# Attention with a gated GLU, forward and backward: one padded weight load per head, and two more natural layouts by crossbar transposes

## The chip, the cores and the metric

The kernel runs on one core of one Trainium2 chip. The metric is the device time of one execution in microseconds (us), as the median of three runs.

## The reference

The forward part normalises x (2048 rows of 576), runs attention of 32 heads over a given cache of 2048 keys and values of width 128, and gates the result:

```python
xn = layernorm(x)
q  = (xn @ wq) per head; p = softmax(q @ k_cache^T * Dh**-0.5); s = (p @ v_cache) @ wo
b  = (sigmoid(xn @ w_gate) * (xn @ w_up)) @ w_down          # F = 4608
out = x + s * silu(b)
```

What is computed is this output and, for a given `grad_out`, the gradients of all of x, k_cache, v_cache, wq, wo, w_gate, w_up and w_down. All inputs and outputs are bf16.

## The kernel before

The program goes through six stages, one after the other.

1. **Gate and up products** (span time 0 to 331 us). The rows stand in 16 row tiles of 128. A loop over (column group, row tile) multiplies a row tile of xn^T by 512 columns of w_gate and w_up at a time and stores the results `h_row` and `a_row` (four buffers each) to DRAM from GpSimd. Beside it runs a "guard": SP loads pieces of k_cache and wq into `x_all`, VectorE and ScalarE square them, and a flag says at the end whether the softmax may leave out its maximum. The order of each engine's instructions here is that of the program.
2. **Down product** (331 to 485): the gate's value and its derivative for each row tile, and dS^T (`dsT`), the gradient before wo. The loads of head 0 start here.
3. **Attention, forward and backward** (485 to 3532). It is made of slots, 32 for each of 32 heads. Slot qt of the first 16 (`main1`) multiplies Q's row tile qt with all keys in two halves and ScalarE exponentiates them into a slab Pq of 128 x 2048; SP turns the slab by a crossbar transpose (`transpose_slab`, line 630). Six slots later (`SKEW`) `tail1` multiplies the turned slab with V. The second 16 slots (`main2`) do the same with dO and V: dP, dS in place of P, a second turn, and `tail2` with K, six slots later. The gradients of V and K are sums over the slabs (`Partial`, line 744) whose stationary operands are dO and Q in natural layout (row on the partition), scaled per row by `scale_don` and `scale_qn`.
4. **Output projection** (3532 to 3677): 16 row tiles; each turns its row of the attention output from DRAM by `load_oT` on SP, into one of three places `oTs`.
5. **GLU backward** (3677 to 4542).
6. **Gradients of wq, wo and x** (4542 to 4945), in eight groups of four heads. SP turns wq's columns (`wqT`) and the rows of dQ (`dqbT`); each group takes eight steps of 32 pairs of matmuls. In the last two groups (`early` and `final`) eight row tiles each of x's gradient are finished between the steps, from step `wait_n` on (`ends_rows`, `finish`); VectorE does most of a finished row. `early` uses also the next group's `wqT2` and `dqbT2`.

Attention takes its order from `plan(h)`: `put(slot, cost, fn)` hangs small units of work on slots, so that the next head is prepared while the last one runs. Before the change these units are, for each head: K and V in four loads each; wo's rows (two loads into `wo_h`) and wq's columns (two loads), all from GpSimd; a crossbar transpose of `wo_h` into `woT` (line 208); four `prep_qt` (Q^T = wq^T xn^T) and four `prep_dot` (dO^T = wo dS^T); crossbar transposes of K and V (`turn_nat`); and two steps that take the natural layouts from the transposed ones on TensorE:

```python
def prep_don(hs, sc):   # four times a head: 4 transposes of 128 x 128, one copy by VectorE
def prep_qn(hs):        # once a head: 16 transposes, two copies by VectorE
```

Both go through `pe_transpose_blocks`, line 145. The attention output and dQ are stored from GpSimd after every fourth row tile (`G4`, `store_nat`, line 677).

Of the kernel before, what the change touches and what calls it, by code (L numbers as in the profile page):

```python
# [9 lines left out]
bf = mybir.dt.bfloat16  # L10
# [3 lines left out]
P = 128  # L14
# [52 lines left out]
def kernel(  # L67
# [41 lines left out]
    dq2_d = dram.tile([S, HD], bf, name="dq2_d")  # L109
    kvT_d = dram.tile([H, 2, P, S], bf, name="kvT_d")  # L110
# [40 lines left out]
    def new_head(h):  # L151
        hs = HeadState()
        hs.h = h
        hs.wq, hs.woT = wqs[h % 2], woTs[h % 2]
        hs.Kn = Kns[h % 2]
        hs.Vn, hs.VT, hs.KT, hs.QT, hs.dOT, hs.dOn, hs.Qn = Vn, VT, KT, QT, dOT, dOn, Qn
        return hs

    def load_wq(hs):
        hcols = slice(hs.h * P, (hs.h + 1) * P)  # L160
        nf = DT - 1 if KPAD else DT
        if nf:
            nc.gpsimd.dma_start(hs.wq[:, :nf, :], A_wq[:nf * P, hcols].rearrange("(i p) c -> p i c", p=P))
        if KPAD:
            nc.gpsimd.dma_start(hs.wq[LO:, nf, :], A_wq[nf * P:, hcols])

    def load_wo(hs):
        nf = (DT - 1) * P if KPAD else D
        rows = slice(hs.h * P, (hs.h + 1) * P)
        if nf:  # L170
            nc.gpsimd.dma_start(wo_h[:, :nf], A_wo[rows, :nf])
        if KPAD:
            nc.gpsimd.dma_start(wo_h[:, nf + LO:], A_wo[rows, nf:])
# [11 lines left out]
    def prep_loads(h):  # L185
        hs = new_head(h)
        load_wq(hs)
        load_wo(hs)
        load_k(hs)
        load_v(hs)  # L190
        return hs
# [8 lines left out]

    def prep_wot(hs):
        pt = acc_tile(bf)
        for i in range(DT):
            nc.tensor.transpose(pt[:, i, :], wo_h[:, i * P:(i + 1) * P], ident[:])
        alt.copy(hs.woT[:], pt[:, :DT, :], eng="s")

    def turn_wot(hs):
        nc.sync.dma_start_transpose(hs.woT[:], wo_h[:])
# [25 lines left out]
    with tc.tile_pool(name="pa", bufs=1) as pa:  # L234
# [75 lines left out]
        with tc.tile_pool(name="a1w", bufs=1) as wp:  # L310
# [37 lines left out]
            with tc.tile_pool(name="a0", bufs=3) as sb0, tc.tile_pool(name="a0ps", bufs=2, space=PSUM) as ps0, \  # L348
# [55 lines left out]

                todo = {"norm": list(range(min(LA + 2, L1), L1)), "turn": list(range(LA, L1)), "bn": list(range(L1, NT))}
# [26 lines left out]
                for n_row, (gi, st) in enumerate(rows_order):  # L432
# [41 lines left out]
                    if gi > 1 and st % 2 and wd_left:  # L474
                        load_wd()
                assert begin is not None
# [4 lines left out]
                while wd_left:  # L481
                    load_wd()
                guard_end()
# [12 lines left out]
        wqs = [pdT.tile([P, DT, P], bf, name=f"wq_h{b}") for b in range(2)]  # L496
        woTs = [pdT.tile([P, DT, P], bf, name=f"woT_h{b}") for b in range(2)]
        for t_ in wqs:
            zlow(t_)
        wo_h = pdT.tile([P, DT * P], bf, name="wo_h")  # L500
        if KPAD:
            nc.gpsimd.memset(wo_h[:, (DT - 1) * P:(DT - 1) * P + LO], 0.0)
# [3 lines left out]
        with tc.tile_pool(name="a2h", bufs=3) as hp, \  # L506
# [49 lines left out]
            prep_wot(heads_pre[0])  # L556
# [31 lines left out]
    G4 = min(4, NT)  # L588
# [4 lines left out]
    def attention(fast):  # L593
        with ExitStack() as es:
# [19 lines left out]
            def turn_nat(dst, src):  # L614
                nc.sync.dma_start_transpose(dst[:].rearrange("p (t q) -> p t q", q=P), src[:].rearrange("p t d -> p (t d)"))

# [170 lines left out]
            def plan(h):  # L787
# [3 lines left out]
                if h:  # L791
                    put(pl, 0, lambda: heads.__setitem__(h, start_head(h)))
                    for c in range(4):
                        put(pl + q(c), 0, lambda c=c: load_k(hd(), c, 4))
                        put(pl + q(skew + 3 + c), 0, lambda c=c: load_v(hd(), c, 4))
                    put(pl + q(4), 0, lambda: load_wo(hd()))
                    put(pl + q(5), 0, lambda: load_wq(hd()))
                    put(pl + q(NTH + 3), 0, lambda: turn_nat(hd().KT, hd().Kn))
                    put(pl + q(skew + 4), 0, lambda: turn_wot(hd()))
                    for sc in range(NSC):  # L800
                        put(pl + q(skew + 4 + 2 * sc), DT * CH, lambda sc=sc: prep_qt(hd(), sc))
# [3 lines left out]
                for sc in range(NSC):  # L805
                    put(b1 + q(sc), DT * CH, lambda sc=sc: prep_dot(hd(), sc))
                    put(b1 + q(sc + 1), nb * P, lambda sc=sc: prep_don(hd(), sc))
                for qt in range(NT):
                    put(b1 + max(qt + 1, q(2 + qt // nb)), 0, lambda qt=qt: scale_don(hd(), qt))
                put(b1 + q(NTH + 3), 0, lambda: turn_nat(hd().VT, hd().Vn))  # L810
                put(b1 + q(NTH + 2), NT * P, lambda: prep_qn(hd()))
# [70 lines left out]
    with late("pc") as pc, late("pcf") as pcf, \  # L882
# [22 lines left out]
        with late("c1l3", 4) as ldp3, late("c1s", 2) as sb, \  # L905
# [34 lines left out]
            for st in range(1, R0):  # L940
                nc.gpsimd.tensor_copy(oTs[st][0:1, 0, 0:1], loads[0][st % 3][0:1, 0:1])
                load_oT(oTs[st], st)
# [217 lines left out]
        with late("c2w") as wp, late("c2b") as blk, late("c2s", 2) as sb, late("c2ps", 4, space=PSUM) as ps:  # L1160
# [45 lines left out]
            for hg in range(NHG):  # L1206
# [6 lines left out]
                for a in range(NTE if final else 0, NT, NQ):  # L1213
                    turn_rows(dqbT, dqb, a, min(a + NQ, NT), HG)
# [4 lines left out]
                wait_n = min(5 if early else 2, nsteps - 2)  # L1219
# [11 lines left out]
                for hl in range(HG):  # L1231
# [4 lines left out]
                    if early and hl == min(1, HG - 1):  # L1236
                        nc.sync.dma_start_transpose(wqT2[:], A_wq[:, (hg + 1) * HC:(hg + 2) * HC])
                        turn_rows(dqbT2, onqs[(hg + 1) % 2][1], 0, NTE, HG)
# [51 lines left out]
```

## Time and profile before

| | |
|---|---|
| median of three runs | 4960.12 us (4959.86 to 4975.73) |
| the profiled execution | 4946.58 us, its span 4944.8 us |
| TensorE busy | 4874.4 us, 99% |
| VectorE, ScalarE, GpSimd busy | 57%, 50%, 17% |
| granted TensorE clock, mean | 0.997 |
| DMA packets under 512 B | 2951889 of 3048180 |
| crossbar transposes of P and dS | 512 and 512, median 5.0 and 5.1 us to landing |

The span runs from the first instruction to the last; the time of an execution includes what lies around it. TensorE's matmuls overlap one another, so that its busy time does not tell how close it is to its pace. The distance between the starts of successive matmuls tells that.

### The profile page before, as it was taken

To read this page: it belongs to the slowest core of one execution; us is meant where nothing else is said; L and a number is where in the kernel's file an instruction comes from. 1 tells how busy PE (TensorE), PEld (TensorE's weight loads), DVE (VectorE), ACT (ScalarE), POOL (GpSimd) and SP (SyncE) were. 2 spreads that over 40 slices of the span, in tenths; PEclk is the share of its full clock that TensorE was granted. 3 is DMA by queue.
4 is the path that set the end of the run, shared out by engine and by line. 5 is a ranking of instruction groups with operands and counts; after the bars stand their busy time and mean duration, and the time that the engine had idled before them with its cause. 6 is when DMAs were issued, how large, how long until landed. Compare 5 with 4: busy or idle time off the path is not lost. (4 is left out here: it accounts for less than half of the span.)

```text
span 4944.8 us, 101626 instructions
## 1 busy us (share of the span) xinstructions
PE 4874.4 (99%) x41029; PEld 2893.5 (59%) x41029; DVE 2801.6 (57%) x6554; ACT 2474.9 (50%) x4228; POOL 842.3 (17%) x1330
## 2 busy tenths in 40 slices
PE   9999999999999999999999999999899999999998
PEld 4445566666666666666666666666455555555554
DVE  4544666666566666666656656666434555553224
ACT  4432666766676676676676667667212111111111
POOL 3322111111111111111111111111221111111111
PEclk9999999999999999999999999999999999999999
DMA  7887999999999999999999999999999999997765
GB/s 260 274 202 175 219 222 227 227 228 226 228 231 226 228 228 232 225 228 229 224 229 231 230 222 231 225 226 231 216 221 238 224 226 223 234 235 185 205 175 131
DMA packets 3048180, 1097.68 MB, mean 222 GB/s; under 512 B 2951889, under 2 KB 2956114, under 8 KB 3047698
## 3 DMA queue, kind: packets, MB, share of 16 engines
q1 hardware_dynamic: 2948930, 771.66, 83.4%
q0 software_dynamic: 98160, 318.85, 20.3%
q8 instruction: 322, 5.28, 0.4%
q14 instruction: 160, 1.31, 0.1%
q10 hardware_dynamic: 608, 0.59, 0.0%
HBM read 175.31 MB, written 177.93 MB: 71 GB/s over the span
## 5 line engine op out<-in xcount | busy, mean ns | idle before, releaser
L654 ACT ACTIVATE Pq<-sp 128x1024 bf16<-128x1024 f32 x1024 | 1048.1, 1024 | 267.2 <-PE sp L636 258.1
L709 DVE SCALAR_TENSOR_TENSOR Pq<-dp,negdelta,Pq 128x1024 bf16<-128x1024 f32 x512 | 654.9, 1279 | 42.9 <-PE dp L706 42.9
L712 ACT ACTIVATE t<-dp,negdelta 128x1024 bf16<-128x1024 f32 x512 | 567.6, 1115 | 214.3 <-PE dp L706 199.8
L636 PE MATMUL sp<-KQ 128*128 128x512 bf16 x2048 | 609.7, 379 | 2.2 <-ACT Pq L654 2.1
L706 PE MATMUL dp<-VT,dOT 128*128 128x512 bf16 x2048 | 609.2, 379 | 2.3
L683 PEld LDWEIGHTS <-dST 128*128 128x128 bf16 x8192 | 508.1, 98 | 150.7 <-DMA dST<-Pq 9.9
L683 PEld LDWEIGHTS <-PT 128*128 128x128 bf16 x8192 | 500.2, 98 | 134.7 <-DMA PT<-Pq 14.0
L683 PE MATMUL acc<-Kn,dST 128*128 128x128 bf16 x8192 | 557.1, 219 | 5.7 <-DMA dST<-Pq 5.7
L683 PE MATMUL acc<-Vn,PT 128*128 128x128 bf16 x8192 | 542.4, 219 | 9.9 <-DMA PT<-Pq 9.6
L713 DVE TENSOR_TENSOR Pq<-t,Pq 128x1024 bf16<-128x1024 bf16 x512 | 354.5, 692 | 316.7 <-ACT t L712 306.2
L744 PE MATMUL acc<-Pq,dOn 128*128 128x512 bf16 x2048 | 531.7, 379 | 0.0
L744 PE MATMUL acc<-Pq,Qn 128*128 128x512 bf16 x2048 | 525.7, 379 | 0.0
L724 ACT ACTIVATE dq_n<-acc,rsc 128x128 bf16<-128x128 f32 x512 | 187.7, 367 | 331.5 <-PE acc L683 310.1
L1153 DVE TENSOR_TENSOR dxn<-acc,dxn 128x576 f32<-128x576 f32 x272 | 206.1, 758 | 248.2 <-PE acc L1053 248.2
L744 PEld LDWEIGHTS <-Qn 128*128 128x128 bf16 x2048 | 200.3, 98 | 240.4 <-issue 0.8
L744 PEld LDWEIGHTS <-dOn 128*128 128x128 bf16 x2048 | 199.0, 98 | 234.2 <-DVE dOn L669 0.3
L1115 ACT ACTIVATE ndh<-dh 128x512 bf16<-128x512 f32 x144 | 86.0, 597 | 452.5 <-DVE du_blk L1113 448.7
L641 DVE TENSOR_REDUCE rs_all<-rsp 128x1 f32<-128x2 f32 x512 | 78.3, 153 | 307.3 <-ACT Pq L654 295.8
L636 PEld LDWEIGHTS <-KQ 128*128 128x128 bf16 x2048 | 179.2, 98 | 124.1 <-issue 3.9
L706 PEld LDWEIGHTS <-dOT 128*128 128x128 bf16 x2048 | 178.7, 98 | 124.2 <-issue 11.7
L677 POOL DMA_DIRECT2D on_d<-o_n x128 | 97.3, 760 | 784.8 <-DVE junk L695 460.3
L677 POOL DMA_DIRECT2D dq_d<-dq_n x128 | 98.1, 766 | 716.9 <-ACT dq_n L724 677.1
(209 smaller groups left out, 6820.8 us busy)
## 6 DMA issues: line engine op xcount, KB each, us to landing
out_dram<-kvn POOLq DMA_DIRECT2D x64, 512.0 KB, 4.6
ah<-a_d POOLq DMA_DIRECT2D x18, 1024.0 KB, 9.5
ah<-h_d POOLq DMA_DIRECT2D x18, 1024.0 KB, 12.1
h_d<-h_row POOLq DMA_DIRECT2D x64, 256.0 KB, 3.4
a_d<-a_row POOLq DMA_DIRECT2D x64, 256.0 KB, 3.8
x_all<-in_A_k_cache_dram SPq DMA_DIRECT2D x64, 256.0 KB, 3.7
on_d<-o_n POOLq DMA_DIRECT2D x128, 128.0 KB, 4.7
kvT_d<-KQ POOLq DMA_DIRECT2D x32, 512.0 KB, 5.5
```

Of the source, the lines that this page charges most:

```text
L636: nc.tensor.matmul(sp[:, c * CH:(c + 1) * CH], lhsT=hs.QT[:, qt * P:(qt + 1) * P], rhs=hs.KT[:, hf * HW_ + c * CH: hf * HW_ + (c + 1) * CH ...
L654: nc.scalar.activation(Pq[:, hsl], sp[:], AF.Exp, scale=SCALE, accum_out=hs.rsp[:, hf:hf + 1])
L677: nc.gpsimd.dma_start(dst_d[q0 * P:(qt + 1) * P, hs.h * P:(hs.h + 1) * P].rearrange("(t p) d -> p t d", p=P), buf[:])
L683: nc.tensor.matmul(hs.acc[:, 0, :], lhsT=T[:, kt, :], rhs=rhs[:, kt, :], start=(kt == 0), stop=(kt == NT - 1))
L706: nc.tensor.matmul(dp[:, c * CH:(c + 1) * CH], lhsT=hs.dOT[:, qt * P:(qt + 1) * P], rhs=hs.VT[:, hf * HW_ + c * CH: hf * HW_ + (c + 1) * C ...
L709: nc.vector.scalar_tensor_tensor(Pq[:, hsl], dp[:], hs.negdelta[:, qt:qt + 1], Pq[:, hsl], op0=ALU.add, op1=ALU.mult)
L712: nc.scalar.activation(t[:], dp[:], AF.Identity, bias=hs.negdelta[:, qt:qt + 1], scale=1.0)
L713: nc.vector.tensor_tensor(Pq[:, hsl], t[:], Pq[:, hsl], op=ALU.mult)
L724: nc.scalar.activation(hs.dq_n[:, qt % G4, :], hs.acc[:, 0, :], AF.Copy, scale=hs.rsc[:, qt:qt + 1])
L744: nc.tensor.matmul(self.acc, lhsT=self.nat[:, qt, :], rhs=self.slabs[qt][:, cs], start=(qt == self.lo), stop=(qt == self.hi - 1))
L1115: nc.scalar.mul(ndh[:], dh[:], -1.0)
L1153: nc.vector.tensor_tensor(dxn[:, st, :], acc[:, :D], dxn[:, st, :], op=ALU.add)
```

## The change

- A DRAM copy `w2_d` holds, for each head, wq's columns and the transposed rows of wo, padded to 5 x 128. It is made in stage 1: `w2_load` brings two heads' wq by GpSimd and turns wo's rows by SP out of DRAM, and one call later `w2_store` clears the padding and stores both. The calls come after every second row from row 18 on. In attention one load per head (`load_w2`) takes the place of four loads and the turn of `wo_h`; head 0's transposes of wo on TensorE go too.
- K and V of the next head are loaded in two halves, not four quarters.
- The attention output and dQ are stored after every eighth row tile.
- `prep_don` and `prep_qn` go. `turn_T` makes dO (in two halves, in slots 2 and 4) and Q (in slot 9) in natural layout by crossbar transposes on SP. `scale_don` starts two slots after its half.
- In the output projection, GpSimd's one-element copy that held back `load_oT` of row tile 1 goes; that for row tile 2 stays.
- In the last stage `early` turns `wqT2` and `dqbT2` ahead of the second half of its own rows, and the final rows start at step 3 (before: 5) and 1 (before: 2).

```diff
-    def load_wq(hs):
...
-    def load_wo(hs):
...
+    def load_w2(hs):
+        nc.gpsimd.dma_start(hs.w2[:], w2_d[hs.h])
...
-    def turn_wot(hs):
-        nc.sync.dma_start_transpose(hs.woT[:], wo_h[:])
...
+                def w2_load():
+                    if w2_left:
+                        hh = w2_left.pop(0)
+                        n = len(hh)
+                        t_ = sb0.tile([P, 2, 2, DT, P], bf, name="w2", bufs=2)
...
+                        for k in range(n):
+                            hc = slice(hh[k] * P, (hh[k] + 1) * P)
+                            if nf2:
+                                nc.gpsimd.dma_start(t_[:, k, 0, :nf2, :], A_wq[:nf2 * P, hc].rearrange("(i p) c -> p i c", p=P))
+                                nc.sync.dma_start_transpose(t_[:, k, 1, :nf2, :], A_wo[hc, :nf2 * P])
+                            if KPAD:
+                                nc.gpsimd.dma_start(t_[LO:, k, 0, nf2, :], A_wq[nf2 * P:, hc])
+                                nc.sync.dma_start_transpose(t_[:, k, 1, nf2, :], A_wo[hc, D - P:])
+                        w2_wait.append((t_, hh))
+
+                def w2_store():
...
+                            nc.gpsimd.memset(t_[:LO, :n, :, nf2, :], 0.0)
+                        nc.gpsimd.dma_start(w2_d[hh[0]:hh[-1] + 1].rearrange("h p k i c -> p h (k i c)"),
+                                            t_[:, :n].rearrange("p h k i c -> p h (k i c)"))
...
+                    if n_row > NT and n_row % 2 == 0:
+                        w2_store()
+                        w2_load()
...
-            prep_wot(heads_pre[0])
...
-    G4 = min(4, NT)
+    G4 = ldiv(NT, 8)
...
+            def turn_T(dst, src, lo, hi):
+                nc.sync.dma_start_transpose(dst[:, lo:hi, :], src[:, lo * P:hi * P])
...
-                    for c in range(4):
-                        put(pl + q(c), 0, lambda c=c: load_k(hd(), c, 4))
-                        put(pl + q(skew + 3 + c), 0, lambda c=c: load_v(hd(), c, 4))
-                    put(pl + q(4), 0, lambda: load_wo(hd()))
-                    put(pl + q(5), 0, lambda: load_wq(hd()))
+                    for c in range(2):
+                        put(pl + q(2 * c), 0, lambda c=c: load_k(hd(), c, 2))
+                        put(pl + q(skew + 3 + 2 * c), 0, lambda c=c: load_v(hd(), c, 2))
+                    put(pl + q(4), 0, lambda: load_w2(hd()))
...
-                    put(pl + q(skew + 4), 0, lambda: turn_wot(hd()))
...
-                    put(b1 + q(sc + 1), nb * P, lambda sc=sc: prep_don(hd(), sc))
+                NDON = 2 if NSC % 2 == 0 else 1
+                for c in range(NDON):
+                    put(b1 + q((c + 1) * NSC // NDON), 0, lambda c=c: turn_T(hd().dOn, hd().dOT, c * NT // NDON, (c + 1) * NT // NDON))
                 for qt in range(NT):
-                    put(b1 + max(qt + 1, q(2 + qt // nb)), 0, lambda qt=qt: scale_don(hd(), qt))
+                    put(b1 + max(qt + 1, q((qt * NDON // NT + 1) * NSC // NDON + 2)), 0, lambda qt=qt: scale_don(hd(), qt))
...
-                put(b1 + q(NTH + 2), NT * P, lambda: prep_qn(hd()))
+                put(b1 + q(NTH + 1), 0, lambda: turn_T(hd().Qn, hd().QT, 0, NT))
...
-                nc.gpsimd.tensor_copy(oTs[st][0:1, 0, 0:1], loads[0][st % 3][0:1, 0:1])
+                if st > 1:
+                    nc.gpsimd.tensor_copy(oTs[st][0:1, 0, 0:1], loads[0][st % 3][0:1, 0:1])
                 load_oT(oTs[st], st)
...
-                for a in range(NTE if final else 0, NT, NQ):
-                    turn_rows(dqbT, dqb, a, min(a + NQ, NT), HG)
+                def turn_dq(a, b):
+                    for a_ in range(a, b, NQ):
+                        turn_rows(dqbT, dqb, a_, min(a_ + NQ, b), HG)
+                turn_dq(NTE if final else 0, NTE if early else NT)
+                if early:
+                    nc.sync.dma_start_transpose(wqT2[:], A_wq[:, (hg + 1) * HC:(hg + 2) * HC])
+                    turn_rows(dqbT2, onqs[(hg + 1) % 2][1], 0, NTE, HG)
...
-                wait_n = min(5 if early else 2, nsteps - 2)
+                wait_n = min(3 if early else 1, nsteps - 2)
...
                     if early and hl == min(1, HG - 1):
-                        nc.sync.dma_start_transpose(wqT2[:], A_wq[:, (hg + 1) * HC:(hg + 2) * HC])
-                        turn_rows(dqbT2, onqs[(hg + 1) % 2][1], 0, NTE, HG)
+                        turn_dq(NTE, NT)
```

## The prediction

> **What bounds the kernel now.** I read the page's first parts, then the busy times by stage, then the waits of TensorE, then its timeline inside one head.
>
> ```profile
> span 4944.8 us, 101626 instructions
> PE 4874.4 (99%) x41029; PEld 2893.5 (59%) x41029; DVE 2801.6 (57%) x6554; ACT 2474.9 (50%) x4228; POOL 842.3 (17%) x1330
> ```
>
> The same by stage, attention, output projection and the last stage:
>
> ```profile
> 485.00:3532.00 3047.00, 3026.33 (x26854) 1896.27 (x26851) 1941.78 (x5152) 2062.05 (x3518) 445.25 (x713) 1.00 1.16 227
> 3532.00:3677.00 145.00, 131.41 (x1094) 69.27 (x1095) 36.98 (x61) 17.50 (x45) 39.30 (x71) 0.96 0.91 208
> ...
> 4542.00:4945.00 403.00, 381.31 (x3078) 195.57 (x3075) 131.95 (x234) 54.46 (x80) 60.42 (x93) 0.98 0.63 172
> ```
>
> After each window's length stand the busy times of PE, weight loads, VectorE, ScalarE and GpSimd, then the granted clock, the DMA share and GB/s. PE idles 70 us in all. Attention (485 to 3532) has 21 us of that in 3047 and the full clock, while ScalarE and VectorE stand at 68% and 64%: an instruction that leaves PE there comes off the time, as long as nothing that replaces it arrives late. The sharper holes are elsewhere, in the waits of PE at the start of the output projection and in the last 125 us:
>
> ```profile
> PE acc L957 <- DMA xnT<-on_d: 10.8, 1, 10.8
> ...
> PE acc L1053 <- DMA dqbT<-dqb: 3.9, 1, 3.9
> PE acc L1053 <- DVE dxn L1256: 2.8, 1, 2.8
> PE acc L1053 <- DVE tot L1192: 2.2, 1, 2.2
> ```
>
> "Busy" is no proof of full pace, so I take the pace from starts. Line 145 holds the transposes that the change takes away; the second fence is the timeline of one slot.
>
> ```profile
> L145 PE MATMUL acct<-ident,dOT x512: 217/219/230, 488.0 to 3436.5; 128*128 128x128 bf16 x171
> L145 PE MATMUL acct<-ident,KQ x512: 218/219/219, 513.4 to 3451.8; 128*128 128x128 bf16 x171
> ```
>
> ```profile
> 2007.90 0.59 PE L636 MATMUL sp<-KQ 128*128 128x512 bf16 x2
> 2008.33 0.39 PE L145 MATMUL acct<-ident,dOT 128*128 128x128 bf16 x4
> 2008.56 0.81 PE L215 MATMUL acc<-dsT,woT_h 128*128 128x512 bf16 x3
> ```
>
> A transpose lasts 219 ns from start to end, but four of them push the next matmul only 0.23 us back: 56 ns each. That, not 219, is what one costs a full PE.
>
> **What the Trainium skill says.** "TensorE: Matmul & The Clock Gate", section "Wait — 56ns, not 53.3ns?", puts back-to-back starts of 128 columns at 55.6 ns when warm; the 0.23 us for four agrees. Its section "What's actually happening" says that an idle window of about 3.4 us halves the clock; the trace agrees in kind: around 3480 to 3570, which holds the 10.8 us wait, the granted clock averages 0.92. "DMA: Bandwidth & Descriptors", section "Latency and other measured facts", gives crossbar transposes 261 GB/s where the middle dimension is strided and 350 to 400 where contiguous. Here, while eight slabs and V^T are turned back to back (2034 to 2052), the GB/s row sits at 290 for most slices, and I use that. Its section "Issuing engines are not separate DMA queues" says that all queues share 16 DMA engines; that matters in the first stage below.
>
> **Part 1, attention: transposes leave PE.** Per head 16 transposes of dO^T (`prep_don`) and 16 of Q^T (`prep_qn`) go: 32 x 32 x 56 ns = **-57 us**, all on the path. With them go VectorE's copies out of PSUM (128 x 425 ns and 64 x 682 ns, 98 us), worth nothing by themselves, since VectorE is at 64% behind PE. In their place SP issues three transposes a head, half a slab of dO twice and a whole slab of Q, and drops the one of wo^T. What is queued behind them on SP are the P^T and dS^T slabs, for which PE waits six slots later.
>
> ```profile
> GB/s 286 236 240 36 271 290 291 266 290 52 0 9 76 290 290 282 291 290 290 374 264 290 291 289 199 269 290 271 224 271 263 290 286 207 278 280 275 225 265 254
> ```
>
> ```profile
> q1 hardware_dynamic: 2106111, 530.84, 102.9%
> ```
>
> ```profile
> L630 SPq DMA_TRANSPOSE PT<-Pq x512: 1416/2160/6704, 490.3 to 3475.6; - x171
> ```
>
> These are the GB/s row of 2034 to 2052, SP's DMA queue over 600 to 3400, and SP's issues of P^T (shortest, median, longest ns). A slab of 128 x 2048 bf16 is 0.524 MB, 1.8 us at 290 GB/s. Now 530.84 MB in 2800 us is 190 GB/s, 65% of the pace. Afterwards a head has 32 slabs, K^T, V^T and two more, 36 x 0.524 = 18.9 MB in 93.4 us (3047 / 32 = 95.2 now, less 1.8): 202 GB/s, 70%. SP's share: an issue takes 1.4 us when nothing holds it, 36 of them 51 us of 93.4; the rest of the median of 2.2 is waiting for slabs. The dO halves fall into slots 2 and 4, where slabs are issued 3.9 us apart (2005.75, 2009.67, 2013.60 in the timeline) and SP waits between; Q falls into slot 9, long after Q^T was made. A slab lands 5.0 us after its issue and is read six slots later, about 17 us at the mean of 95.2 / 32 = 3.0 a slot; an added 1.8 us of crossbar still fits. VectorE's `scale_don` and `scale_qn` wait for the landing and hold what is behind them, but the code leaves two slots (about 6 us) to the former and three to the latter. The cover is that slack; if it fails, every late turn costs PE up to its own 1.8 us. No row shows these turns in place, so I bound them: 0 below (what a wait frees was counted already), 3.6 us a head or **+115 us** above. I take **+2**.
>
> K and V in halves, one weight load and stores of eight tiles remove DMA issues from GpSimd, at 15% of attention (and its 383 us wait for `wo_h`). No PE wait ends on them: 0. The larger store buffers move nothing before the next stages, which read them much later: 0. The five PE transposes of `prep_wot` for head 0 are 0.3 us: 0.
>
> **Part 2, first stage: the padded copy is made.** Sixteen steps of two heads each load wq (four GpSimd DMAs) and turn wo (four SP transposes, 1.2 us each by the issue of woT), then a memset and a store. They start in row 18, about 77 us, at every second row; by row 50 (about 200 us) all are through.
>
> ```profile
> 77.00:200.00 123.00, 123.00 (x572) 55.75 (x570) 63.28 (x99) 55.66 (x100) 41.07 (x73) 1.00 0.79 271
> ```
>
> 33.4 MB move there now. Added: 4.7 MB of wq, 4.7 of wo and, padded to 640 columns, 10.5 of stores, 19.9 together; 53.3 MB in 123 us is 433 GB/s. The weight loads of 10 to 50 us ran at 349 on average, with slices over 400. So the engines are short by 0 us (at 433) to 30 us (at 349). Behind this GpSimd holds the stores of `h_row` and `a_row`, of which there are four buffers (some 13 us of rows), and SP holds the guard loads, seven pieces ahead of their squares. Most of the shortage is absorbed there. GpSimd's own time is no bound: 41 us of 123 plus 16 x about 3.6 (four loads and a store at 0.55 to 0.75 us each, a memset). PE stands still between 0 and +30 us; I take **+8**.
>
> **Part 3, output projection.** Row tile 1's transpose no longer waits for GpSimd's gating copy. It was issued at 3539.26 and landed at 3549.2; without the gate SP may begin once attention is left, about 3535. The weights loaded by GpSimd from 3540 on contend less with it, but the next wait (2.1 us for row tile 2, still gated) grows. Gain between 0 and 11; I take **-5**.
>
> **Part 4, last stage.** The group before last turns the next group's rows before its own second half and starts final rows at step 3, not 5; the last starts at step 1, not 2. A step is 32 matmul pairs, 3.92 us; a final row occupies VectorE for 4.35 us (in the timeline its rows start that far apart), more than PE needs for one. An earlier start thus removes the 2.2 and 2.8 us waits, and the half clock near them. What is late next: rows at step 3 need `dqbT2` at about 4837, and three SP issues stand before it, so a wait of about 4 us stays; in the last group rows at step 1 wait some 3 us for `dqbT`. Between +6 and -10; I take **-4**.
>
> **Sum.** -57 + 2 + 8 - 5 - 4 = -56. The profiled execution takes 4946.6 (span 4944.8 and 1.8 around it), so 4890 for such a one. The median of the runs is 4960.1, 13.5 more; I carry that over: **4904 us**.
>
> **Rivals.** (a) The first stage is short by its whole 30 us and the last stage loses 6: -57 + 2 + 30 - 5 + 6 = -24, **4936**. For it: 433 against 349 GB/s and GpSimd waiting for landings in order; against it: buffers of rows and pieces. (b) **Slower**: the crossbar queue. If each head's three turns reach SP while it is already behind, P^T or dS^T arrives after its slot, PE waits the turn's own time, and 3.6 us a head less the 1.8 saved gives +58, with the rest -1: **5017**. It decides at 1.8 us of new waiting per head. For it: in slots 10 to 25 SP issues with 0.09 us between, and the DMA share is already 1.16. Against it: 65% to 70% of the crossbar's own pace, and under 16 us of PE waits on slabs in the whole run. (c) Another engine takes over: ScalarE's two exps need 2 x 1.02 us and part of 2 x 0.19 for their sums, about 2.2 of a mean slot's 3.0; if it bound, little of the 57 would show, about **4955**. That the turn is compiled to something else is excluded: K and V take the same path now.
>
> **Numbers.** Main case 0.72, (a) 0.12, (b) 0.12, (c) 0.04. A measurement of this kernel can tell about 0.3%, 15 us. Main and (a) are faster: 0.84; (c) same, with a little of the main case: 0.05; slower 0.11. The main case alone spans 4882 (all gains at their ends) to 4930; the range reaches on to (a) and a partial (b), 4880 to 4948.
>
> **What would show it.** Line 145 has 16 matmuls left; attention takes about 2990 us; PE's waits on PT and dST stay under some 40 us in all; in 77 to 200 us PE busy falls below the window by about 8. Waits of PE on PT or dST of 60 us and more, or new VectorE waits on dOn and Qn that PE echoes, would prove (b). If the span to the first exp (485 now) grows by over 20, it is (a).

## The result: 4% slower, and the profile after

The change costs 4%: 5168.94 us median (5153.12 to 5178.91) against 4959.99 (4953.28 to 4975.73) in the runs beside it, ratio 1.0414, 95% interval 1.0377 to 1.045. The profiled execution takes 5165.98 us, against 4946.58. The first two lines of its page, and TensorE's transposes:

```profile
span 5164.2 us, 98914 instructions
...
PE 4895.7 (95%) x40000; PEld 2871.6 (56%) x40000; DVE 2694.8 (52%) x6362; ACT 2471.8 (48%) x4227; POOL 702.9 (14%) x1074
```

```profile
L146 PE MATMUL pt<-ident,Kn x16: 219/219/220, 538.5 to 539.4; 128*128 128x128 bf16 x16
```

The change does what it says: the 16 left are those of head 0's K, the others are gone from TensorE (line 146 of the changed kernel is line 145 of the one before). Yet TensorE is busy for longer, with fewer instructions. By stage (a window of stage 1 that holds most of the new copy, then attention, output projection, last stage; columns as in the prediction's windows):

```profile
77.00:200.00 123.00, 105.07 (x462) 45.85 (x460) 46.07 (x74) 39.41 (x74) 70.72 (x115) 0.96 1.04 281
545.00:3756.00 3211.00, 3028.97 (x25836) 1870.24 (x25834) 1836.89 (x4960) 2063.58 (x3519) 246.19 (x372) 0.98 1.14 225
3756.00:3903.00 147.00, 136.49 (x1094) 70.85 (x1095) 36.87 (x60) 17.96 (x46) 39.13 (x70) 0.94 0.88 205
4768.50:5164.00 395.50, 380.18 (x3070) 195.52 (x3068) 131.64 (x233) 54.29 (x80) 60.50 (x93) 0.98 0.67 174
```

Stage lengths from the first matmul of each stage to the first of the next, in us:

| | gate and up | down | attention | output proj. | GLU backward | last |
|---|---|---|---|---|---|---|
| before | 331.3 | 151.9 | 3048.9 | 145.4 | 865.4 | 401.9 |
| after | 388.6 | 156.2 | 3211.3 | 146.9 | 865.4 | 395.7 |
| difference | +57.3 | +4.3 | +162.4 | +1.5 | 0 | -6.2 |

The differences add up to 219.3, the whole of it. Attention should have become 57 us shorter and became 162 longer. TensorE's waits in the whole run name the place:

```profile
PE acc L693 <- DVE junk L705: 161.8, 31, 9.7
PE g_ps L456 <- ACT a_row L463: 42.5, 17, 4.7
...
PE acc L693 <- DMA dST<-Pq: 9.6, 6, 4.7
PE acc L1064 <- DMA dqbT<-dqb: 7.2, 2, 4.3
...
PE acc L693 <- DMA PT<-Pq: 6.0, 4, 4.9
```

31 waits of 5.2 us in the mean, one in each head but the first, for `junk`, the VectorE instruction that frees the accumulator in PSUM. TensorE hardly waits for PT and dST, so late slabs are not the reason here. VectorE's own waits say what holds `junk`:

```profile
DVE Qn L682 <- DMA Qn<-KQ: 273.3, 32, 13.2
```

Once in each head VectorE stands for the landing of Qn, 8.5 us in the mean. The timeline of one head, from start, length and engine to the wait before in brackets:

```profile
2071.53 0.28 DVE L705 SCALAR_TENSOR_TENSOR junk<-acc,dOn 128x128 f32<-128x128 f32 x1
...
2071.74 0.08 DVE L705 DVE_READ_ACCUMULATOR junk<-acc,dOn 128x1 f32 x1
...
2073.86 2.19 SPq L625 DMA_TRANSPOSE Qn<-KQ  x1
...
2076.15 2.89 SPq L640 DMA_TRANSPOSE PT<-Pq  x1
...
2079.28 1.23 DVE L682 TENSOR_SCALAR Qn<-Qn,rinv_all 128x128 bf16<-128x128 bf16 x7 [7.46 <-DMA Qn<-KQ]
...
2081.78 1.47 PE L693 MATMUL acc<-Vn,PT 128*128 128x128 bf16 x13 [4.01 <-DVE junk L705]
```

After the `junk` of 2071.5 the next instructions in VectorE's queue are seven `scale_qn`. The plan puts these in slots 12 to 15; in the order in which the engine runs them, in every head but the first, seven of the sixteen stand between the row sums of slot 7 and those of slot 8, ahead of the next `o_n` and `junk`. The turn has moved up too: the plan puts it in slot 9, SyncE issues it ahead of P^T of slot 7. It is issued at 2073.86, behind three P^T turns, and lands at about 2079. VectorE stands for 7.46 us, the accumulators fill, TensorE stops for 4.0 us. In the kernel before, the same `scale_qn` came after two copies out of PSUM that TensorE's transposes had just filled, and never waited.

The stop costs more than itself. The granted clock is at half for 160 us of attention, against 7 before. The Trainium skill, "TensorE: Matmul & The Clock Gate", section "What's actually happening", says that an idle window of some 3.4 us sets the clock to half. The trace agrees, the clock being the third number from the end (the stop of 4.0 us, then the time after it):

```profile
2077.80:2081.80 4.00, 0.02 (x1) 0.02 (x1) 2.47 (x16) 1.11 (x2) 0.00 (x0) 1.00 1.24 264
2081.90:2085.30 3.40, 3.40 (x21) 2.22 (x20) 2.68 (x14) 0.84 (x1) 0.00 (x0) 0.50 1.20 251
```

The run `qn_pool` below has the same matmuls without this stop, and 48 us at half clock: TensorE is busy for 2976.9 us there, 52 less than the 3029.0 here. Half of the 112 us between the two is 56, so the clock can account for these 52 us (an estimate from the two traces).

### The profile page after: what moved, and what is told of

It reads as the page before. It is cut to its first block, busy times and chain, and to the rows that moved or that the text cites. A ratio compares the mean times of both kernels' runs of the same rounds, so it can differ in the third digit from the quotient of the medians.

```text
span 5164.2 us, 98914 instructions
## 1 busy us (share of the span) xinstructions
PE 4895.7 (95%) x40000; PEld 2871.6 (56%) x40000; DVE 2694.8 (52%) x6362; ACT 2471.8 (48%) x4227; POOL 702.9 (14%) x1074
## 4 chain that ended last, share of the span: by engine, by line
PE 84%; DMA 8%; DVE 3%; issue 2%; SPq 1%; POOL 1%; ACT 1%; POOLq 0%; ACTq 0%
PE acc L693 17%; PE acc L754 16%; PE acc L1008 12%; PE dp L716 8%; PE sp L646 8%; PE acc L1064 8%; PE acc L194 5%; DMA Qn<-KQ 3%; PE dh L1121 3%; PE acc L968 2%; PE acc L541 2%; PE u_ps L458 1%; PE g_ps L456 1%; DVE Qn L682 1%; DVE Pq L719 1%
## 5 line engine op out<-in xcount | busy, mean ns | idle before, releaser
L693 PE MATMUL acc<-Vn,PT 128*128 128x128 bf16 x8192 | 564.5, 224 | 167.8 <-DVE junk L705 161.8
L693 PEld LDWEIGHTS <-PT 128*128 128x128 bf16 x8192 | 520.8, 100 | 300.1 <-issue 176.1
L646 PE MATMUL sp<-KQ 128*128 128x512 bf16 x2048 | 626.8, 388 | 1.2 <-ACT Pq L664 1.0
L754 PE MATMUL acc<-Pq,dOn 128*128 128x512 bf16 x2048 | 549.2, 389 | 0.0
L682 DVE TENSOR_SCALAR Qn<-Qn,rinv_all 128x128 bf16<-128x128 bf16 x512 | 110.8, 249 | 273.3 <-DMA Qn<-KQ 273.3
L716 PEld LDWEIGHTS <-dOT 128*128 128x128 bf16 x2048 | 178.8, 98 | 124.2 <-issue 11.1
L456 PE MATMUL g_ps<-wg_sb,xnT 128*128 128x512 bf16 x720 | 186.4, 391 | 42.5 <-ACT a_row L463 42.5
## 6 DMA issues: line engine op xcount, KB each, us to landing
x_all<-in_A_k_cache_dram SPq DMA_DIRECT2D x64, 256.0 KB, 10.4
```

The costliest lines, as they stand in the source:

```text
L456: nc.tensor.matmul(g_ps[:], lhsT=xnT[:, i, srows], rhs=wg_sb[:, i, fs], start=(i == 0), stop=(i == DT - 1))
L646: nc.tensor.matmul(sp[:, c * CH:(c + 1) * CH], lhsT=hs.QT[:, qt * P:(qt + 1) * P], rhs=hs.KT[:, hf * HW_ + c * CH: hf * HW_ + (c + 1) * CH ...
L693: nc.tensor.matmul(hs.acc[:, 0, :], lhsT=T[:, kt, :], rhs=rhs[:, kt, :], start=(kt == 0), stop=(kt == NT - 1))
L716: nc.tensor.matmul(dp[:, c * CH:(c + 1) * CH], lhsT=hs.dOT[:, qt * P:(qt + 1) * P], rhs=hs.VT[:, hf * HW_ + c * CH: hf * HW_ + (c + 1) * C ...
L754: nc.tensor.matmul(self.acc, lhsT=self.nat[:, qt, :], rhs=self.slabs[qt][:, cs], start=(qt == self.lo), stop=(qt == self.hi - 1))
```

## The experiments

Two theories: **V**, VectorE's wait for the landing is all that attention loses (theory 1 in the first expectations); **Q**, beside it each turn added to SyncE's queue makes P^T late. I measure them by the slots: the time from a slot's first exponential to the next slot's (slot 15 ends where VectorE begins the second half), as a mean over heads 2 to 30, less that of the kernel before, in us for each head. The kernel before has 94.77.

| | slots 0-9 | 10 | 11 | 12-15 | second half | sum |
|---|---|---|---|---|---|---|
| after | -0.89 | -0.88 | +6.86 | -0.03 | +0.05 | +5.11 |
| qn_pe | -0.89 | +0.17 | +0.15 | +0.28 | +0.89 | +0.59 |
| qn_pool | -0.89 | -0.72 | +0.36 | +3.07 | +1.65 | +3.47 |
| no_w2 | -0.89 | -0.89 | +8.18 | -0.02 | +0.03 | +6.40 |
| don_only | -0.85 | +0.06 | +0.31 | +1.19 | +0.23 | +0.93 |
| don_act | +6.95 | 0 | -0.07 | +1.23 | +0.23 | +8.34 |
| don_sk7 | +0.23 | 0 | 0 | +0.75 | +0.65 | +1.63 |
| qn_two | +2.79 | -0.81 | +0.21 | +0.68 | +0.47 | +3.34 |
| qn_two_pin | +0.27 | -0.20 | +0.07 | +1.22 | +1.01 | +2.38 |
| spare_turns | 0 | +0.02 | 0 | +1.28 | +0.27 | +1.57 |
| best_qn | 0 | -0.89 | +0.01 | +2.88 | +0.11 | +2.11 |
| best_all | 0 | -0.89 | 0 | +2.54 | +0.78 | +2.43 |
| don_light | -0.89 | 0 | 0 | -0.08 | -0.06 | -1.04 |
| rest | 0 | 0 | 0 | +0.34 | +0.65 | +1.00 |
| last_only | 0 | 0 | 0 | +0.04 | +0.01 | +0.06 |

The second set of numbers that matters is how long after the end of a slot's last exponential its P^T lands (median over heads 2 to 31, of those turns whose landing the trace holds):

| P^T of slot | 2 | 4 | 6 | 8 | 9 | 11 | 14 |
|---|---|---|---|---|---|---|---|
| before | 4.1 | 3.8 | 9.0 | 11.0 | 10.8 | 10.3 | 9.3 |
| after | 4.0 | 9.4 | 10.7 | 14.4 | 14.1 | 7.7 | 6.7 |
| don_only | 6.4 | 10.3 | 12.8 | 14.0 | 15.1 | 13.3 | 11.7 |
| qn_pool | 5.4 | 11.0 | 11.6 | 15.7 | 16.1 | 16.0 | 11.9 |
| spare_turns | 6.7 | 6.1 | 11.8 | 14.1 | 15.1 | 12.9 | 11.4 |
| best_qn | 8.0 | 6.1 | 12.4 | 15.4 | 15.8 | 13.8 | 12.2 |
| don_light | 4.2 | 4.3 | 8.7 | 7.7 | 8.1 | 6.5 | 5.9 |

In the kernel before TensorE begins to read the turn of slot 8 13.6 us after the end of slot 8's exponentials, and that of slot 9 after 14.1 (medians). So a landing at 11 is in time, and one at 14 or 15 is not. In the changed kernel itself 14.4 is harmless: with the stop of slot 11 in between, TensorE comes to this turn only after 19.2 us.

**1. `qn_pe`: the changed kernel with Qn back on TensorE.**

```diff
-put(b1 + q(NTH + 1), 0, lambda: turn_T(hd().Qn, hd().QT, 0, NT))
+put(b1 + q(NTH + 2), NT * P, lambda: prep_qn(hd()))
```

> The changed kernel with Q's natural layout made on TensorE again (prep_qn in slot 10); the two halves of dO still go through the crossbar. Theory 1, VectorE stands in order behind the landing of Q's turn and PE is stopped by its full accumulators: attention falls from 3211 us to 3049 - 32 x 16 x 56 ns = about 3020, the run to about 4978. Theory 2, the crossbar and SP are overloaded by the added turns: half of the added volume stays, so about half of the 220 us of loss stays, attention near 3130, the run near 5090.

Measured: 5034.77 (5021.11 to 5044.48), ratio 1.0164 (1.014 to 1.0189); attention 3064.0. Removing the turn of Qn takes 134 us off, so it is the largest loss; but attention should be 3049 - 28.5 = 3020, and 44 us are missing. For these the turns of dO (run 3) and the K and V loads in halves (runs 14 and 15) come in question; this run holds both.

**2. `qn_pool`: the changed kernel with `scale_qn` on GpSimd.**

```diff
-nc.vector.tensor_scalar(hs.Qn[:, qt, :], ...
+nc.gpsimd.tensor_scalar(hs.Qn[:, qt, :], ...
```

> The changed kernel with one word different: scale_qn runs on GpSimd, so that VectorE never waits for Q's turn. Crossbar, SP and the transposes are as in the changed kernel. Theory 1 (VectorE's order): the 273 us of VectorE waits on Q and the 162 us of PE waits on junk go, attention about 2990, the run about 4950. Theory 2 (crossbar and SP): no change, attention 3211, the run 5169.

Measured: 5108.33 (5075.93 to 5111.48), ratio 1.0288 (1.0245 to 1.0331); attention 3151.4. GpSimd takes the wait over, and TensorE now waits for slabs:

```profile
POOL Qn L682 <- DMA Qn<-KQ: 361.7, 32, 16.1
```

```profile
PE acc L693 <- DMA PT<-Pq: 108.1, 88, 4.3
...
PE acc L693 <- DMA dST<-Pq: 35.6, 23, 4.5
```

VectorE's wait is gone, but only 61 us of the 209 that the change costs go with it. Both gains stand in the table (-0.89 in the slots of dO, -0.72 in slot 10), and slots 12 to 15 and the second half take 4.7 us a head. So V alone does not hold; something stands behind it.

**3. `don_only`: the kernel before with dO's turns as the only change** (`scale_don` in the slots that the change gives it).

```diff
-put(b1 + q(sc + 1), nb * P, lambda sc=sc: prep_don(hd(), sc))
+put(b1 + q((c + 1) * NSC // NDON), 0, lambda c=c: turn_T(hd().dOn, hd().dOT, ...))
```

> The kernel before with only dO's natural layout by two crossbar turns. Theory 1: VectorE's waits on dO are short (48 us in the changed kernel) and PE does not see them: attention 3049 - 29 = 3020, the run about 4931. Theory 2: a third to a half of the 220 us loss shows, the run 5000 to 5040.

Measured: 4981.66 (4976.59 to 4992.13), ratio 1.0053 (1.0036 to 1.0069). The part that I thought safest loses too:

```profile
PE acc L686 <- DMA PT<-Pq: 37.3, 44, 2.3
PE acc L686 <- DMA dST<-Pq: 11.4, 15, 3.8
```

In the kernel before:

```profile
PE acc L683 <- DMA PT<-Pq: 9.6, 6, 3.6
PE acc L683 <- DMA dST<-Pq: 5.7, 5, 3.0
```

15 us on slabs before, 49 now. P^T of slots 4 to 9 lands 3 to 6.5 us later. SyncE's issues of the two kinds of turn (shortest, median, longest, ns):

```profile
L618 SPq DMA_TRANSPOSE dOn<-dOT x64: 1247/1286/4482, 495.6 to 3470.1; - x64
L633 SPq DMA_TRANSPOSE PT<-Pq x512: 1422/2290/8520, 490.7 to 3506.8; - x171
```

From the end of one issue to the end of the next it takes some 1.4 us for a dO turn (8 blocks) and 2.0 to 2.4 (quartile and median) for a P^T or dS^T turn (16 blocks), while slots 5 to 9 come every 2.3 to 3.1 us. A queue that runs this near to its limit carries each added microsecond on for many slots. VectorE waits 117 us for the landing of dOn, which is new too, so the cause is not yet told apart.

**4. `no_w2`: the changed kernel without the copy of the weights** (loads and turn of wo as before; stores of four row tiles, to make room).

> The changed kernel without the padded copy: wq and wo per head as before, stores of four row tiles because the buffers of eight do not fit beside it. Theory 3, stage 1 loses 57 us because the copy's DMAs crowd out the stores of h_row and a_row: stage 1 back to 331 us, the run about 5108. Rival, something else that differs in stage 1: stage 1 stays above 370. Attention keeps its loss, 3211, under theory 1; if the weight load per head had a part in it, attention moves by more than 20 us.

Measured: 5138.34 (5135.26 to 5144.39), ratio 1.0367 (1.0342 to 1.0392). Stage 1 is 331.0 again and the down product 151.9: the copy's whole cost is 57.3 + 4.3. But the total falls by 31 only. The turn of wo is on SyncE again, VectorE waits 301 us for Qn, not 273, and attention grows to 3248.9.

**5. `don_act`: `don_only` with the two dO turns issued from ScalarE** (`nc.scalar` in place of `nc.sync`).

> The kernel before with dO turned by the crossbar, as in the earlier run of that part alone (4982 us), except that the two turns of a head are issued from ScalarE's queue and not from SyncE's. Theory Q (the bound is SyncE's in-order queue, which needs some 2.0 to 2.4 us for each P^T or dS^T turn while slots of the P half come every 2.3 to 2.6 us; each dO turn ahead of them takes 1.37 us of it): with the two turns gone from SyncE, P^T lands as in the kernel before (11 us after its last exponential at worst, not 14 to 15), TensorE's waits on PT and dST fall from 49 us to about 15, and the gain of 16 transposes x 56 ns x 32 heads = 29 us shows: about 4930 us, 4945 if ScalarE pays for the 1.3 us of each issue in its slots. Theory X (the crossbar transfers themselves slow each other, whoever issues them): P^T stays late, 4975 to 4990 us.

Measured: 5213.4 (5212.27 to 5252.16), ratio 1.0535 (1.049 to 1.058); attention 3309. Neither figure. ScalarE, in slot 2 of a head, and SyncE's waits for dO's landing in the whole run (L633 issues the P^T and dS^T turns, L208 that of wo):

```profile
1520.96 0.19 ACT L657 ACTIVATION_READ_ACCUMULATOR Pq<-sp 128x1 f32 x1
1526.31 1.25 ACTq L618 DMA_TRANSPOSE dOn<-dOT  x1
1527.68 0.37 ACT L727 ACTIVATE dq_n<-acc,rsc 128x128 bf16<-128x128 f32 x1 [6.53 <-issue]
```

```profile
SPq L633 <- DMA dOn<-dOT: 191.6, 35, 7.3
SPq L208 <- DMA dOn<-dOT: 157.1, 29, 7.1
```

ScalarE stands for 5.2 us between its last work and the issue, and the exponentials wait behind it; the issue itself takes 1.25 us. The trace shows what it waits for: SyncE's last turn lands at 1526.02, ScalarE's is issued at 1526.31 and lands at 1529.42, SyncE's next is issued at 1529.47. It is so in all 64 cases: no turn of SyncE is seen in flight when ScalarE's is issued, and SyncE waits 349 us for dO's landings. As built, the program never has turns of the two queues in flight together. So this run measures that alternation and says nothing on the question it was built for, whether the queue or the transfers behind it are the limit.

**6. `don_sk7`: `don_only` with SKEW 7 instead of 6.**

> The kernel before with dO turned by the crossbar from SyncE's queue, and SKEW 7 instead of 6: each P^T and dS^T product runs one slot (2.3 to 3.7 us) later behind its exponentials. Theory Q (P^T is late by the 2 to 3 us that two dO turns add to SyncE's queue, against a slack of six slots, about 15 us): one more slot of slack covers it, TensorE's waits on PT and dST fall below 20 us, about 4930 us. Rival: TensorE stands because the slots of that stretch have no work left in them, or because VectorE waits for the landing of dOn; then one slot more changes nothing, 4975 to 4990 us, or 4960 if half of it is so.

Measured: 5006.94 (5001.33 to 5026.46), ratio 1.0106 (1.0078 to 1.0135). A miss: waits on slabs are 45 us, not under 20. The issue of a turn also ends later now, 7.3 us after its exponential already in slot 2 (2.4 before). The eight slab buffers `wpt` are a likely reason, since each is held one slot longer, but that was not tried. New is a wait of TensorE on `dOT`, 28.5 us, while VectorE waits 204 us for dOn.

**7. `qn_two`: the changed kernel, a second Qn buffer, turn in slot 1 instead of 9.**

```diff
+hs.Qn = Qn_odd if h % 2 else Qn
-put(b1 + q(NTH + 1), 0, lambda: turn_T(hd().Qn, hd().QT, 0, NT))
+put(b1 + q(1), 0, lambda: turn_T(hd().Qn, hd().QT, 0, NT))
```

> The changed kernel with a second Qn buffer and the turn of Qn in slot 1 of the P half instead of slot 9 (the stores are of four row tiles, to make room). Stage 1 keeps its extra 57 us and the last stage its 6 us gain. Theory 1 (VectorE's hoisted scale_qn waiting for the landing is all that the attention stage loses): attention is 3049 - 57 = 2992 us, total about 4955 us. Theory Q (behind that wait stands SyncE's queue: a Qn turn takes 2.3 us of it and the two dO turns 1.4 us each): VectorE's wait on Qn goes, but TensorE waits on PT and dST for 100 us and more, as in the run with scale_qn on GpSimd, attention 3080 to 3150 us, total 5045 to 5115 us. If nothing but the place of VectorE's wait changes: 5140 to 5170 us.

Measured: 5113.25 (5102.53 to 5119.67), ratio 1.03 (1.0276 to 1.0325); attention 3152.8. The stop moves along with the turn: +3.04 in slot 2, where VectorE now waits (216 us in 32 waits for Qn's landing, 16 in each buffer). Here each `scale_qn` stands right behind its own row sum, so the first ones stand ahead of the landing again.

**8. `qn_two_pin`: the same, the first eight scales held back to slot 8** by reading a copy `rq` of the row factors that needs the eighth row.

```diff
+put(b1 + q(NTH + 1), 0, lambda: nc.vector.tensor_copy(hd().rq[:], hd().rinv_all[:, :NTH]))
-..., hs.rinv_all[:, qt:qt + 1], None, op0=ALU.mult)
+..., (hs.rq if qt < NTH else hs.rinv_all)[:, qt:qt + 1], None, op0=ALU.mult)
```

> As the run with a second Qn buffer and the turn in slot 1, and in addition the scales of Qn's first eight tiles read a copy of the row factors that is made only once the eighth row is there, so that they can't stand in VectorE's queue before slot 8. Theory: what that run lost in slots 2 and 3 (3.2 us a head, VectorE waiting for the landing of Qn behind hoisted scales) goes, about 100 us: attention near 3050 us, total 4995 to 5025 us from 5113, of which 57 to 60 us are still stage 1. Rival: the crossbar queue takes what VectorE gives back, total 5060 to 5100 us.

Measured: 5079.46 (5075.35 to 5091.52), ratio 1.0249 (1.023 to 1.0268). The stop of slot 2 is gone (-0.22, as it should be), yet only 34 of the expected 100 us come back. TensorE's waits in it:

```profile
PE acc L697 <- DMA PT<-Pq: 51.5, 49, 3.8
...
PE acc L697 <- DMA dST<-Pq: 28.2, 19, 3.9
PE acc L697 <- DVE dOT L42: 24.7, 13, 5.8
```

The dO turns stand behind the Qn turn now, VectorE waits 187 us for dOn, and P^T is late. The rival was right.

**9. `spare_turns`: the kernel before, nothing removed, two turns more for each head that nobody needs.** This tells Q from VectorE's waiting.

```diff
+put(b1 + q(2 * c + 2), 0, lambda c=c: nc.sync.dma_start_transpose(spare[:], hd().dOT[:, c * NTH * P:(c + 1) * NTH * P]))
```

> The kernel before with nothing taken away: two more turns of 8 blocks per head, of dO^T into a spare buffer that nobody reads, are issued from SyncE in slots 2 and 4, where the turns of dO stood in the run of that part alone. VectorE waits for none of it. Theory Q (the loss of the dO part is SyncE's queue, 1.37 us for each such turn): P^T lands 2 to 3 us later in slots 4 to 9 (14 us after the last exponential, not 11), TensorE's waits on PT and dST rise from 15 us to 35 to 60, total 4975 to 5000 us; the 16 transposes per head are still on TensorE, so nothing is gained back. Rival D (that loss was VectorE's wait for the landing of dOn, 117 us in that run): no change, 4953 to 4965 us.

Measured: 5015.7 (5002.04 to 5024.73), ratio 1.012 (1.0103 to 1.0137). TensorE's waits:

```profile
PE acc L688 <- DMA PT<-Pq: 39.5, 38, 2.3
...
PE acc L688 <- DMA dST<-Pq: 14.7, 12, 5.2
```

Nobody waits for these turns, and P^T of slots 8 and 9 lands at 14.1 and 15.1, as in `don_only`. The median is 57 us above the kernel before, more than expected; in the profiled execution it is 55, of which 50 are attention (1.57 x 32). The delay arises ahead of the landing: SyncE's issue of slot 8's turn ends 11.1 us after the exponentials, not 8.4, and lands 3.0 us after that (2.6 before). So Q is shown, and VectorE isn't needed for it. Whether SyncE's own issuing sets the pace, or the transfers that its queue has to make room for, is not told apart: the shortest issue of a long turn is 1.42 us, its median 2.2.

**10. `best_qn`: the kernel before, only Qn turned, in two turns in slots 1 and 2, upper half double, scales held back as in 8.**

> The kernel before, with dO left on TensorE and only Qn turned by the crossbar: in two turns of 8 blocks in slots 1 and 2 of the P half, where SyncE's queue is shortest (1.7 to 4 us behind), the upper half of Qn with a second buffer, and the scales held back to slot 8 as in the run before this. Theory: SyncE absorbs 2 x 1.37 us there, the 16 transposes x 56 ns = 0.89 us a head are gained in full, 28 us: about 4930 us (4923 to 4942). Rival: any turn more on SyncE shows up as late P^T, 4955 to 4980 us.

Measured: 5009.33 (4999.63 to 5025.89), ratio 1.0095 (1.008 to 1.0111). A miss. The 0.89 of slot 10 is there, no VectorE wait for Qn, but slots 12 to 15 give 2.88 back: PE waits 76.9 us on PT. SyncE is only 3.6 to 4 us behind in slots 4 and 5, but by slot 8 it is 12.3, against 8.4 before. The room that I saw in slots 1 and 2 does not last.

**11. `best_all`: the same with K and V in halves and the edits of the output projection and the last stage.**

> As the run before this, with the parts of the change that cost nothing so far: K and V loaded in halves and the last stage of the changed kernel (6 us shorter in every run with it); no copy of the weights, dO on TensorE, stores of four row tiles. Theory: 28 + 6 us, about 4924 us (4915 to 4937). Rival: as above, 4950 to 4975 us.

Measured: 5008.13 (5005.98 to 5012.98), ratio 1.0097 (1.0082 to 1.0113). The last stage gains (393.1), attention loses it again.

**12. `don_light`: `don_only` with two turns taken off SyncE**.

```diff
+if h < 2:
     put(pl + q(skew + 4), 0, lambda: turn_wot(hd()))
+if h < 1:
     put(b1 + q(NTH + 3), 0, lambda: turn_nat(hd().VT, hd().Vn))
```

> The run with the dO part alone (4982 us), with two turns of the P half left out of SyncE's queue: wo^T is turned for the first two heads only and V^T for the first only, so later heads multiply old wo^T and V^T; everything else is issued as before. That takes 1.4 + 2.2 us a head off SyncE, against the 2 x 1.37 us that the dO turns added. Theory Q: P^T lands at slots 8 and 9 as in the kernel before (11 us after the last exponential) or sooner, TensorE's waits on PT fall from 37 us to under 10, and the 29 us that TensorE no longer spends on transposes show: 4925 to 4940 us. If the loss sits elsewhere (in VectorE's 117 us of waiting for dOn, or in slots with too little work): 4965 to 4985 us.

Measured: 4953.98 (4948.31 to 4960.8), ratio 0.9992 (0.9984 to 1.0001). From head 2 on every head takes 93.7 us against 94.6 or more, and TensorE's waits on PT are

```profile
PE acc L686 <- DMA PT<-Pq: 7.9, 6, 2.4
```

with 7.3 of the 7.9 within the first two heads. So the whole gain of dO's transposes comes back when SyncE has room: -1.04 a head. That the total is only 2 us below, and not in the range expected, lies in heads 0 and 1, which take 115.1 and 103.4 us against 89.9 and 94.6: 34 us. In the second half of head 0 ScalarE stands 11.5 us for the store of `o_n`, in slot 2 of head 1 9.5 us for that of `dq_n`; why these stores are late I have not followed up.

**13. `w2_plain`: the changed kernel with the turns of wo in stage 1 replaced by plain loads of the same bytes**.

> The changed kernel with the wo turns of stage 1 replaced by plain loads of the same rows and bytes, so wo^T holds wo untransposed; the rest is the same. Theory T (the crossbar turns out of DRAM in stage 1 hold the DMA engines up and lengthen every landing there): stage 1 is back to 331 to 345 us from 389, total about 5115 us. Rival V (it is the volume, 19 MB read and 19 MB written, or the loads of wq in 256-byte pieces): stage 1 stays at 375 to 390 us, total 5150 to 5170 us.

Measured: 5128.8 (5125.16 to 5140.44), ratio 1.0342 (1.0317 to 1.0367). Stage 1 takes 351.4. Of the 57.3 us that the changed kernel loses there, 37.2 go with the turns out of DRAM; 20.1 are the bytes and the remaining transfers. What holds stage 1 in the changed kernel is ScalarE, which from 77 us on waits until a buffer of `a_row` has been stored (99.1 us in this run, not once in the kernel before):

```profile
ACT a_row L463 <- DMA a_d<-a_row: 116.3, 26, 9.3
```

The guard loads of k_cache on SyncE show how landings lengthen: the kernel before, the changed kernel, this run (last column: us to landing):

```profile
x_all<-in_A_k_cache_dram SPq DMA_DIRECT2D x64, 256.0 KB, 3.7
```

```profile
x_all<-in_A_k_cache_dram SPq DMA_DIRECT2D x64, 256.0 KB, 10.4
```

```profile
x_all<-in_A_k_cache_dram SPq DMA_DIRECT2D x64, 256.0 KB, 7.0
```

GpSimd also waits in order for the turns to land before it stores the copy (14.8 us in nine waits), and its stores of `a_row` and `h_row` stand behind that; how much of the 37 us is this was not tried.

**14. `rest`: what is left of the change without new turns and without the copy** (K and V in halves, the edits of the output projection and the last stage).

> The changed kernel with dO and Qn back on TensorE, without the copy of the weights and with stores of four row tiles: what is left of the change is K and V loaded in halves and the last two stages' edits. Theory: no turn is added to SyncE, so attention is as before (3049 us), the last stage is 6 to 9 us shorter as in every run with those edits: 4950 to 4953 us. Rival: the loads in halves make dS^T late (the three runs that had them on top of the extra turns waited 20 to 23 us on dST, not 10 to 15): 4958 to 4970 us.

Measured: 4968.33 (4952.89 to 4979.17), ratio 1.0019 (1.0009 to 1.0029). The rival was right: the last stage is 7 us shorter, but PE waits 20 us on dST and attention is 3076.7.

**15. `last_only`: the edits of the output projection and the last stage alone.**

> The kernel before with the edits of the output projection and of the last stage alone; K and V in quarters again. Theory: the loads in halves were what made dS^T late in the run before this one (attention 3077 us, 28 above the kernel before); without them attention is 3049 us again and the 6 to 9 us of the last stage show: 4948 to 4953 us. Rival: attention differs by 10 to 30 us between builds for other reasons: 4956 to 4970 us.

Measured: 4943.33 (4938.93 to 4945.78) against 4953.34, ratio 0.9978 (0.9969 to 0.9987): the median is 10 us below the kernel before; the interval leaves out 1.

```profile
483.00:3533.00 3050.00, 3005.14 (x26385) 1896.27 (x26865) 1942.15 (x5153) 2059.97 (x3519) 446.31 (x716) 1.00 1.15 227
3533.00:3683.00 150.00, 134.17 (x1076) 70.83 (x1096) 37.47 (x61) 18.07 (x46) 38.61 (x70) 0.94 0.88 201
4548.00:4943.00 395.00, 374.55 (x3007) 193.63 (x3066) 131.34 (x233) 53.85 (x80) 60.34 (x93) 0.99 0.65 174
```

Attention is as before, the last stage 6.4 us shorter (395.5 against 401.9), the output projection 4.6 longer in this execution. The only difference from `rest` in what runs is the size and the slots of the K and V loads, so these halves cost 25 us between the two medians, or some 20 by the two ratios to the kernel before. How they make dS^T late is open.

## Why the prediction was wrong

- **The gain of 57 us was right.** Every run in which a group of 16 transposes leaves TensorE shows -0.88 or -0.89 in its slots where nothing stops it, against 16 x 56 ns = 0.90. The pace from starts, not the 219 ns of one, was the right price.
- **The failed step is the +2 for waits behind the landings**: "the code leaves two slots (about 6 us) to the former and three to the latter". The slot in which the plan puts a unit of work does not fix its place in an engine's queue. Seven `scale_qn`, planned for slots 12 to 15, stood ahead of the row sums of slot 8, and VectorE held `junk`, `o_n` and the row sums for 7.5 us in the head shown. In place of +2 the term measured +6.86 a head in slot 11, some 219 us over 32 heads: attention is 162 longer where it should have been 57 shorter. (That the whole kernel is 219 us slower as well is chance: the other terms cancel.) `qn_two` and `qn_two_pin` show the cause: the stop goes where the turn goes, and it is gone once the scales are held back (both with the turn in slot 1; slot 9 with the scales held back was not run).
- **The crossbar's cover was misjudged as well.** "A slab lands 5.0 us after its issue and is read six slots later" counts from the issue. That median is the same after (4.9) and says nothing of what stands before it: in the kernel before, P^T of slot 8 already lands 11 us after its exponentials and is read at 13.6, not at 17. And the 65 to 70% of the crossbar's pace are a mean over a head; slots 5 to 9 come every 2.3 to 3.1 us, hardly slower than the 2.0 to 2.4 us from issue to issue. Rival (b) had this mechanism, and its price is of the right size: 1.8 us a head for dO's two turns, where `don_only` loses 1.8 (+0.93, and a gain of 0.89 that does not show); 3.6 for all three, where `qn_pool` loses 5.2. In the changed kernel it is hidden behind VectorE's stop: TensorE waits 15.6 us for slabs in the whole run, so the sign "under some 40 us" came true although attention lost. (b) also said that VectorE waits "that PE echoes" would prove it; those were a cause of their own, as `spare_turns` shows the queue without them.
- **Stage 1, +8 with an upper bound of 30, measured +57.3** (and +4.3 in the next stage). This is rival (a), at twice its price; its sign came true, the first exponential being 62 us later (57.3 + 4.3). The mechanism (short engines, everything behind waits for landings) was right, the size was not: 433 or at least 349 GB/s were assumed, from plain loads. In 77 to 200 us the engines move 281 with a DMA share of 1.04, and 336 in `w2_plain`. The turns out of DRAM were priced by bytes like copies; they are 37 of the 57.
- **K and V in halves, 0: wrong**, 20 to 25 us between `rest` and `last_only`. No wait of TensorE ended on these loads, and yet their size bears on dS^T.
- **Output projection, -5: wrong.** Row tile 1's wait of 10.8 us is gone, but TensorE still idles for 10.5 us there against 14, partly for the weights, and the clock is at half for 17 us of the stage, not 10. The stage is no shorter (146.9 after, 150.0 in `last_only`, 145.4 before).
- **Last stage, -4: right**, -6.2 and -6.4: the waits of 2.2 and 2.8 us for finished rows are gone, the one for `dqbT` has grown from 3.9 to 7.2.

## What to carry to other kernels

Before work goes from a full engine to a queue, measure that queue at its worst stretch: from the moment its input is ready, not from the issue, to the landing, against the time at which it is read. In a pipeline that is ordered in advance, ask of each instruction that will wait for the new transfer what stands behind it in its engine's queue, and fix its place by a dependence and not by the slot in the plan. A small turn that nobody needs, added to the old kernel, prices a queue without any other change.

## What the runs showed of the hardware

- Two crossbar turns of 8 blocks for each head, each taking SyncE 1.35 us from end to end and read by nobody, cost 50 us over 32 heads, 1.57 us a head, though the mean load of the queue looked like two thirds. The shortest issue is 1.25 us for 8 blocks and 1.42 for 16; whether the 2.0 to 2.4 us between long turns is then the issue itself or waiting for room in the queue was not separated.
- An issue of a turn takes ScalarE 1.25 us as well. With turns in both queues the program let those in flight land first, 64 times of 64, and SyncE waited 349 us for it.
- After a stop of 4.0 us TensorE's clock was granted at half for 3.4 us. A stop of 3.1 us was followed by half clock too, stops of 2.7 and 2.9 us were not. Against `qn_pool`, 112 us more of attention at half clock go with 52 us more of TensorE's time for the same matmuls.
- In stage 1 the 64 turns out of DRAM and the copies with them raised the landing of 256 KB loads beside them from 3.7 to 10.4 us; with plain loads of the same bytes in place of the turns it was 7.0.
